# Moving a weight split from the last 33 attention steps into the last ten, and two of its operations to GpSimd

## The chip, the cores and the metric

The kernel runs on one core of one Trainium2 chip. The metric is device time in microseconds (us). The kernel before takes 701.96 us, the median of 3 runs that lie between 701.85 and 702.72.

A core has five engines that each work through an instruction queue of their own, in order, and wait for one another through semaphores: PE (TensorE, matmuls and transposes), DVE (VectorE), ACT (ScalarE), POOL (GpSimd) and SP (SyncE, which here only issues DMA transfers).

## The reference, cut to what matters

```
# attention: 2 batches x 8 heads, 1152 keys, 64 per head, queries averaged in pairs (576)
q_pool = q.reshape(B, H, S // 2, 2, D).mean(axis=3)
attn   = softmax(q_pool @ k.T / sqrt(D))            # with + 1e-09 in the denominator
x      = (attn @ v), heads side by side             # 1152 tokens x 512
# first feed-forward layer (d_ff 2048)
h = x @ w_in
x = where(h > 0, h, exp(min(h, 0)) - 1) @ w_out
# second feed-forward layer (d_ff 1536)
xn  = x / sqrt(mean(x * x) + 1e-06) * rms_g
out = (silu(xn @ w_gate) * (xn @ w_val)) @ w_out2
```

The weights are float64 in DRAM. The kernel reads each as pairs of 32-bit words and builds a float32 from them with integer and float operations; each float32 is then split into a high and a low part, and a product is three matmuls (high by high, low by high, high by low).

## The kernel before

**Attention** runs in 72 steps: eight pairs of heads p (0 to 7) by nine query tiles i (0 to 8). Step n issues, in this order:

- PE: the score matmuls of tile n into the PSUM tile `s` (L279, 6 matmuls, 12 for tile 2 of each p, which serves both heads). There is one `s` buffer, so they wait until DVE has read the scores of tile n-1.
- DVE: `p` (L283), which copies the scores out of `s` and takes their minimum.
- PE: nine transposes of the probabilities of tile n-2 into three PSUM banks `t` (L297). For each bank ACT casts the high part out (`pth`, L305), then DVE subtracts it (`ptl`, L69). There are only three banks, so the transposes of step n+1 wait for the casts and subtractions of step n.
- PE: up to eight matmuls of probabilities by values (L323).
- ACT: the exponential of tile n (L288).
- POOL: the preparation of a later head's q, k or v (`do_prep`), followed by SP's DMA of the next one (`fetch`). The k halves and the v tiles share two buffers (tag `raw`), so SP's DMA for one waits until POOL is done with the tile two places earlier.
- last, `ws.step`, which takes operations from the weight stream.

**The weight stream** (class `Stream`) hands out one operation for each `next`. For a piece of 128 x 512 weights these are, in order: the ACT operation A (`wt`, L113) on the high words; e (`we`, L115) on the low words; then the rest of the piece before it (a marker, the ACT copy of its high part `wh` L141, its low part `wl` on POOL L63); the clamp (L120); the shift (L122); the sign (L124), after which the load of a further piece is issued; and the integer add (L128). That is nine steps of the stream for a piece. The raw words are in two buffers (`wr`, loaded in L90 by SP); `load` issues a piece's DMA ahead, but the first two loads are issued in the same place as the first A. Three pieces can be split before the attention buffers are freed; the stream then stops by itself.

The stream is advanced by L500, one operation in each of the last 33 attention steps, so the three pieces and the float32 of a fourth are built over steps 39 to 71. After attention `early` multiplies with the three pieces, and `elu` advances the stream by two operations at two places of each tile.

The order of every engine's queue is the order in which the program issues; nothing reorders it.

Of the kernel before, what the change touches and what calls it, by code (L numbers as in the profile page):

```python
# [11 lines left out]
ALU = mybir.AluOpType  # L12
# [12 lines left out]
LEAST64, MOST64 = 2.0 ** -18, float.fromhex("0x1.dffffep+13")  # L25
# [13 lines left out]
def tile_kernel(ctx: ExitStack, tc: tile.TileContext, qd, kd, vd, w1d, w2d, wgd, wvd, wod, rgd, outd):  # L39
    nc = tc.nc  # L40
    V, G, T, PE, SP = nc.vector, nc.gpsimd, nc.scalar, nc.tensor, nc.sync
    ctx.enter_context(tc.manual_schedule())
    f = lambda a: a.bitcast(F32)
# [27 lines left out]
    NE, WB = 3, 8  # L71

    class Stream:
# [23 lines left out]
        def work(self):  # L97
            tail = None
            for i in range(len(self.srcs)):
                if tail and not wide:  # L100
                    yield from tail
                self.load(i + 2)
                w = self.raw.pop(i)
                if wide:

                    lo, hi = w[:, :, 0], w[:, :, 1]  # L110
                    e = wp.tile([128, 512], U32, tag="we", name="we", bufs=2)
                    t = wp.tile([128, 512], U32, tag="wt", name="wt", bufs=2)
                    T.activation(out=f(t), in_=f(hi), func=AF.Abs, scale=0.125)  # L113
                    yield
                    V.tensor_scalar(out=f(e), in0=lo, scalar1=2.0 ** -27, scalar2=2.0 ** 25,  # L115
                                    op0=ALU.mult, op1=ALU.add)
                    yield
                    if tail:
                        yield from tail
                    V.tensor_scalar(out=f(t), in0=f(t), scalar1=LEAST64, scalar2=MOST64, op0=ALU.max, op1=ALU.min)  # L120
                    yield
                    V.tensor_scalar(out=t, in0=t, scalar1=3, scalar2=None, op0=ALU.logical_shift_left)  # L122
                    yield
                    V.scalar_tensor_tensor(out=t, in0=hi, scalar=0x80000000, in1=t,  # L124
                                           op0=ALU.bitwise_and, op1=ALU.bitwise_xor)
                    self.load(i + 3)
                    yield
                    V.tensor_tensor(out=t, in0=t, in1=e, op=ALU.add)  # L128
                    w = f(t)
                tail = self.split(i, w)  # L130
                yield
            yield from tail
# [135 lines left out]
    def emit_S(p, i):  # L268
        if i == 0:
            st[p] = ap.tile([128, 4, NPT, 1], F32, tag="st", name="st", bufs=2)  # L270
        s = (tp if (p, i) == (0, 1) else sp).tile([128, 3, 512], F32, tag="s", name="s", bufs=1)
        if i == M:
            parts = [(QD[p, j][:, u, c:c + 128], KD[p, j]) for j, c in ((1, 0), (0, 576)) for u in (0, 1)]
        else:
            j, c, _, _, _ = TILES[i]
            parts = [(QD[p, j][:, u, c:c + 128], KD[p, j]) for u in (0, 1)]
        for n, (a, b) in enumerate(parts):
            for m in range(3):
                PE.matmul(s[:, m, 0:384], lhsT=a, rhs=b[:, 384 * m:384 * m + 384],  # L279
                          start=n == 0, stop=n == len(parts) - 1)  # L280
        pt = P[p, i] = ap.tile([128, 3, 384], F32, tag="p", name="p", bufs=3)

        V.tensor_scalar(out=pt, in0=s[:, :, 0:384], scalar1=-0.0625, scalar2=None,  # L283
                        op0=ALU.mult, op1=ALU.min, accum_out=st[p][:, 0, TILES[i][4], :])

    def emit_exp(p, i):
        pt = P[p, i]
        T.activation(out=pt, in_=pt, func=AF.Exp, scale=-1.0, bias=st[p][:, 0, TILES[i][4], :],  # L288
                     accum_out=st[p][:, 1, TILES[i][4], :])
# [57 lines left out]
    def emit_r(p):  # L347
        s = st[p]
        V.tensor_scalar(out=s[:, 2], in0=s[:, 1], scalar1=1e-9, scalar2=None, op0=ALU.add)
        V.reciprocal(s[:, 3], s[:, 2])  # L350
        hi_pool(rs, s[:, 3, 0:8].to_broadcast([128, 8, 64]))

    def emit_scale(p):

        s, x = st[p], xf[p]
        rb, rm = tbank(), tbank()
        for k in range(4):
            PE.transpose(rb[:, 128 * k:128 * k + 128], rs[:, 2 * k:2 * k + 2, :].rearrange("p a b -> p (a b)"), ident)
        PE.transpose(rm[:, 0:128], s[:, 3, 8, :].to_broadcast([128, 128]), ident)
        xs = ap.tile([128, QS], F32, tag="xs", name="xs", bufs=1)  # L360
        for a, b in ((0, 0), (320, 256)):
            T.copy(xs[:, a:a + 256], rb[:, b:b + 256])
        for j in range(2):
            r = slice(64 * j, 64 * j + 64)
            T.copy(xs[r, 256:320], rm[r, r])
        return xs

    def emit_x(p, xs, a=0, b=QS):
        x = xf[p][:, a:b]
        n, c = divmod(p, 4)  # L370
        h, l = (t[:, c, n * QS + a:n * QS + b] for t in (xh, xl))
        if p < 7:
            G.tensor_tensor(out=x, in0=x, in1=xs[:, a:b], op=ALU.mult)
            hi_pool(h, x)
            lo_pool(l, x, h)
        else:
            V.tensor_tensor(out=x, in0=x, in1=xs[:, a:b], op=ALU.mult)
            T.copy(h, x)
            lo_dve(l, x, h)
# [4 lines left out]
    ws = Stream(w_in[:NE] + [w for hf in range(2) for w in  # L384
                             (w_in[8:16] if hf else w_in[NE:8]) + [w_out[4 * (2 * hf + q) + m] for m in range(4) for q in range(2)]]
                + [w[i] for i in range(12) for w in (wgd, wvd)] + [wod[i] for i in range(12)])
# [4 lines left out]
    def do_prep(u, eng):  # L391
        {"q": prep_q, "k": prep_k, "v": prep_v}[u[0]](*u[1:], raws.pop(u), eng)
# [3 lines left out]
    def fetch(u):  # L396
        if u not in raws:
            raws[u] = load(*u)
# [6 lines left out]
    ns = len(steps)  # L405
# [11 lines left out]
    t = ap.tile([128, 3, 384], F32, tag="p", name="rawq0", bufs=3).rearrange("p a b -> p (a b)")  # L417
    t = t.rearrange("p (u c) -> p u c", u=2)
# [31 lines left out]
    def do_T(step):  # L450
        pt, it = steps[step - LT]
        if avq and any(overwrites(it, a.g) for a in avq):
            assert not any(overwrites(it, a.g) for a in avq[1:])
            avq[0].emit(18)
        emit_T(pt, it)

    def do_AV(k, then):
        while k and avq:
            k -= avq[0].emit(k)
            if avq[0].n < 18:  # L460
                break
            a = avq.pop(0)
            a.finish()
            if a.g is GROUPS[3]:
                then(a.p)

    def after_T(step):
        pt, it = steps[step - LT]
        seen.add((pt, it))
        for g in GROUPS:  # L470
            if it in g["tiles"] and all((pt, t) in seen for t in g["tiles"]):
                avq.append(AV(pt, g))

    for step in range(ns):
        emit_S(*steps[step])
        if step == 1:
            tctx.close()
            tp = actx.enter_context(tc.tile_pool(name="psT", bufs=1, space=PSUM))
            tbank = lambda: tp.tile([128, 512], F32, tag="t", name="t", bufs=3)

        due = [w for w in later if w[0] <= step]
        if step >= LT and not due:
            do_T(step)
        for w in due:
            later.remove(w)
            w[1]()
        do_AV(8, lambda p: later.append((step + 2, lambda: emit_x(p, emit_scale(p)))))
        if step >= LT and due:
            do_T(step)
        emit_exp(*steps[step])  # L490
        if step >= LT:
            if steps[step - LT][1] == NPT - 1:
                emit_r(steps[step - LT][0])
            after_T(step)
        for u in jobs.get(step, []):
            do_prep(u, (ACT[0], lo_pool) if step < 4 and u[0] != "q" else POOL)
            n = order.index(u)
            if n + 1 < len(order):
                fetch(order[n + 1])
        ws.step(0, step >= ns - 33)  # L500


    fb = sp.tile([128, 3, 512], F32, tag="s", name="fb", bufs=1)
# [233 lines left out]
```

## Time and profile before

| what | us |
|---|---|
| time of the profiled execution | 702.4 |
| its span, first to last instruction | 700.6 |
| median of the 3 runs | 701.96 |
| PE busy | 682.1 (97%) |
| DVE busy | 546.2 (78%) |
| ACT busy | 416.0 (59%) |
| POOL busy | 374.9 (54%) |

The span is what lies between the first and the last instruction; the reported time has 1.8 us more around it. Busy time is a sum over the whole span, and an engine's share differs between stages: a stage is read from a table of windows or a timeline. The attention steps end at about 250 us, and the first tile after attention (`elu`) starts at 262.6 us.

### The profile page before, as it was taken

The numbers are of one execution on the slowest core, as the hardware profiler recorded it, in microseconds if no ns is written. First come the engines' busy times: TensorE is split into PE (matmuls) and PEld (weight loads), VectorE is DVE, ScalarE is ACT, GpSimd is POOL, SyncE is SP. The second block draws the span as 40 slices with busy tenths as digits, with TensorE's granted clock in tenths as the row PEclk, the third lists the DMA queues.
The fourth block names the chain that finished last, engine by engine and source line by source line (L and its number), as shares of the span: only waits on it lengthen the run. The fifth ranks groups of instructions, "written<-read, shape, count | busy, mean of one in ns | idle before, by whom it ended". The sixth has DMA issues, their size and how long they took to land.

```text
span 700.6 us, 11340 instructions
## 1 busy us (share of the span) xinstructions
PE 682.1 (97%) x4243; PEld 669.4 (96%) x4243; DVE 546.2 (78%) x897; ACT 416.0 (59%) x855; POOL 374.9 (54%) x326
## 2 busy tenths in 40 slices
PE   7999999999999999996999999999999999999997
PEld 6999999989899999996999999999999999999997
DVE  6988889898999967999988999766999876584000
ACT  5988889889887957765447774434444444342000
POOL 3989788897978405765434545442454443342000
PEclk9999999999999999998999999999999999999999
DMA  5423323433432001222442222200323222232000
GB/s 199 123 85 114 124 86 102 145 116 95 143 114 67 1 31 33 89 90 94 148 142 69 70 83 91 90 1 31 121 91 114 96 91 91 90 101 84 35 35 34
DMA packets 21606, 62.33 MB, mean 89 GB/s; under 512 B 2736, under 2 KB 4784, under 8 KB 21552
## 3 DMA queue, kind: packets, MB, share of 16 engines
q1 hardware_dynamic: 21552, 61.62, 26.4%
q8 instruction: 33, 0.54, 0.3%
q14 instruction: 21, 0.17, 0.1%
HBM read 59.25 MB, written 2.36 MB: 88 GB/s over the span
## 4 chain that ended last, share of the span: by engine, by line
PE 81%; DVE 12%; ACT 3%; POOL 1%; DMA 1%; issue 1%; SPq 0%; DVEq 0%; ACTq 0%; POOLq 0%
PE b L168 17%; PE b L167 17%; PE b L169 17%; PE s L279 10%; PE o L323 9%; PE t L297 8%; DVE p L283 3%; DVE ptl L69 2%; DVE wt L124 2%; DVE wt L122 1%; DVE wt L120 1%; DVE e L187 1%; DMA rawk<-in_k_dram 1%; POOL wl L63 1%; DVE wt L128 1%
## 5 line engine op out<-in xcount | busy, mean ns | idle before, releaser
L167 PE MATMUL b<-xh,wh 128*128 128x384 f32 x468 | 157.4, 336 | 0.6 <-ACT sl L638 0.6
L169 PE MATMUL b<-xh,wl 128*128 128x384 f32 x468 | 157.1, 336 | 0.0
L168 PE MATMUL b<-xl,wh 128*128 128x384 f32 x468 | 157.0, 335 | 0.0
L63 POOL TENSOR_TENSOR wl<-wt,wh 128x512 fp32r<-128x512 f32 x68 | 99.8, 1467 | 72.8 <-ACT wh L141 53.8
L283 DVE TENSOR_SCALAR_CACHE_REDUCE p<-s 128x1152 f32<-128x1152 f32 x72 | 97.4, 1353 | 20.0 <-PE s L279 19.9
L69 DVE TENSOR_TENSOR ptl<-t,pth 128x384 fp32r<-128x384 f32 x216 | 106.6, 549 | 2.7 <-ACT pth L305 2.2
L279 PE MATMUL s<-kd,qt 128*128 128x384 f32 x480 | 99.3, 345 | 5.5 <-DVE p L283 3.8
L305 ACT CAST pth<-t 128x384 fp32r<-128x384 f32 x216 | 89.4, 486 | 23.3 <-PE t L297 22.7
L288 ACT ACTIVATE p<-p,st 128x1152 f32<-128x1152 f32 x72 | 91.4, 1269 | 5.8 <-DVE p L283 5.4
L279 PEld LDWEIGHTS s<-kd,qt 128*128 128x128 f32 x480 | 82.8, 191 | 9.1 <-DVE p L283 4.3
L167 PEld LDWEIGHTS b<-xh,wh 128*128 128x128 f32 x468 | 87.9, 188 | 1.1 <-ACT sl L638 0.9
L168 PEld LDWEIGHTS b<-xl,wh 128*128 128x128 f32 x468 | 87.9, 188 | 0.0
L169 PEld LDWEIGHTS b<-xh,wl 128*128 128x128 f32 x468 | 87.9, 188 | 0.0
L297 PE MATMUL t<-ident,p 128*128 128x128 f32 x648 | 85.5, 275 | 0.2 <-DVE p L283 0.2
L113 ACT ACTIVATE wt<-wr 128x512 f32<-128x512 f32 x68 | 46.0, 676 | 66.6 <-POOL wl L63 50.9
L323 PE MATMUL o<-pth,vd 128*128 128x256 f32 (+1 forms) x288 | 84.4, 315 | 0.0
L124 DVE SCALAR_TENSOR_TENSOR wt<-wr,wt 128x512 uint32<-128x512 uint32 x68 | 80.5, 1184 | 1.8
L297 PEld LDWEIGHTS t<-ident,p 128*128 128x128 f32 x648 | 73.9, 141 | 6.6 <-DVE ptl L69 4.0
L323 PE MATMUL o<-ptl,vd 128*128 128x256 f32 (+1 forms) x288 | 78.4, 295 | 0.0
L63 POOL TENSOR_TENSOR gl<-e,gh 128x384 fp32r<-128x384 f32 x37 | 44.9, 1215 | 45.8 <-ACT gh L188 45.8
L128 DVE CUSTOM_DVE_ANT_0 wt<-wt,we 128x1024 uint16<-128x1024 uint16 x68 | 65.8, 968 | 1.9
L167 PE MATMUL b<-gh,wh 128*128 128x384 f32 x180 | 62.0, 344 | 5.2 <-ACT gh L188 4.6
(113 smaller groups left out, 1317.6 us busy)
## 6 DMA issues: line engine op xcount, KB each, us to landing
wr<-in_w_dram SPq DMA_DIRECT2D x32, 512.0 KB, 3.2
rawk<-in_k_dram SPq DMA_DIRECT2D x32, 288.0 KB, 2.9
rawq<-in_q_dram SPq DMA_DIRECT2D x15, 576.0 KB, 4.0
wr<-in_wg_dram SPq DMA_DIRECT2D x12, 512.0 KB, 3.2
wr<-in_wv_dram SPq DMA_DIRECT2D x12, 512.0 KB, 3.2
wr<-in_wo_dram SPq DMA_DIRECT2D x12, 512.0 KB, 3.2
rawv<-in_v_dram SPq DMA_DIRECT2D x16, 288.0 KB, 2.9
out_dram<-o SPq DMA_DIRECT2D x12, 192.0 KB, 1.8
```

Of the source, the lines that this page charges most:

```text
L63: G.tensor_tensor(out=o, in0=i, in1=f(h), op=ALU.subtract)
L69: V.tensor_tensor(out=o, in0=i, in1=f(h), op=ALU.subtract)
L124: V.scalar_tensor_tensor(out=t, in0=hi, scalar=0x80000000, in1=t, op0=ALU.bitwise_and, op1=ALU.bitwise_xor)
L167: PE.matmul(out, lhsT=wh[:, k, :], rhs=ah, start=first and k == 0, stop=False)
L168: PE.matmul(out, lhsT=wh[:, k, :], rhs=al, start=False, stop=False)
L169: PE.matmul(out, lhsT=wl[:, k, :], rhs=ah, start=False, stop=last and k == 3)
L279: PE.matmul(s[:, m, 0:384], lhsT=a, rhs=b[:, 384 * m:384 * m + 384], start=n == 0, stop=n == len(parts) - 1)
L283: V.tensor_scalar(out=pt, in0=s[:, :, 0:384], scalar1=-0.0625, scalar2=None, op0=ALU.mult, op1=ALU.min, accum_out=st[p][:, 0, TILES[i][4], :])
L288: T.activation(out=pt, in_=pt, func=AF.Exp, scale=-1.0, bias=st[p][:, 0, TILES[i][4], :], accum_out=st[p][:, 1, TILES[i][4], :])
L297: PE.transpose(ps[:, k, :], src[:, 128 * b:128 * b + 128], ident)
L305: T.copy(oh, re(ps))
L323: PE.matmul(self.o[:, 0:self.N], lhsT=v[:, b, :], rhs=(pth, ptl)[u][:, g["buf"], b, g["c0"]:320], start=self.n == 0, stop=self.n == 17)
```

## The change

The e operation and the clamp of the first three pieces go to POOL instead of DVE, and the two bounds of the clamp change places. The stream is advanced by three operations in each of the last ten attention steps (62 to 71) instead of by one in each of the last 33. Line numbers behind L116 are one higher in the changed kernel.

```diff
-                    V.tensor_scalar(out=f(e), in0=lo, scalar1=2.0 ** -27, scalar2=2.0 ** 25,
-                                    op0=ALU.mult, op1=ALU.add)
+                    (G if i < NE else V).tensor_scalar(out=f(e), in0=lo, scalar1=2.0 ** -27, scalar2=2.0 ** 25,
+                                                       op0=ALU.mult, op1=ALU.add)
                     yield
                     if tail:
                         yield from tail
-                    V.tensor_scalar(out=f(t), in0=f(t), scalar1=LEAST64, scalar2=MOST64, op0=ALU.max, op1=ALU.min)
+                    (G if i < NE else V).tensor_scalar(out=f(t), in0=f(t), scalar1=MOST64, scalar2=LEAST64,
+                                                       op0=ALU.min, op1=ALU.max)
...
-        ws.step(0, step >= ns - 33)
+        ws.step(0, 3 * (step >= ns - 10))
```

Three places of the order matter. On SP, at the end of the attention's loads (`rawk`, `rawv` and `rawq` are the k, v and q tiles, `wr` the raw words of the weights), there stands before:

```order
L233 DMA rawv<-in_v_dram 128x576
L224 DMA rawq<-in_q_dram 128x1152
L230 DMA rawk<-in_k_dram 128x576 x2
L90 DMA wr<-in_w_dram 128x1024
L233 DMA rawv<-in_v_dram 128x576
L90 DMA wr<-in_w_dram 128x1024 x27
```

and now:

```order
L234 DMA rawv<-in_v_dram 128x576
L225 DMA rawq<-in_q_dram 128x1152
L231 DMA rawk<-in_k_dram 128x576 x2
L234 DMA rawv<-in_v_dram 128x576
L90 DMA wr<-in_w_dram 128x1024 x32
```

Five loads of weights stood between the attention's loads, the first two of them in step 39; now all 32 stand behind the last of them, the v tile of head 7, 0.

On ACT, around the exponential of step 62 (`p`), there stands before, from the casts of step 62 to those of step 64:

```order
L305 CAST pth<-t 128x3x128 x3
L288 ACTIVATE p,st<-p,st 128x1152
L305 CAST pth<-t 128x3x128 x3
L336 COPY olo<-o 64x320
L338 COPY xf<-o 64x320
L288 ACTIVATE p,st<-p,st 128x1152
L113 ACTIVATE wt<-wr 128x512
L305 CAST pth<-t 128x3x128 x3
```

and now:

```order
L306 CAST pth<-t 128x3x128 x3
L289 ACTIVATE p,st<-p,st 128x1152
L113 ACTIVATE wt<-wr 128x512
L306 CAST pth<-t 128x3x128 x3
L337 COPY olo<-o 64x320
L339 COPY xf<-o 64x320
L289 ACTIVATE p,st<-p,st 128x1152
L306 CAST pth<-t 128x3x128 x3
```

The A operation that stood here was that of the fourth piece; the one that stands here now is that of the first, directly behind the exponential of step 62 and ahead of the casts of step 63.

On DVE, from the scores of step 62 to those of step 64, there stands before:

```order
L283 TENSOR_SCALAR p,st<-s 128x1152
L69 TENSOR_TENSOR ptl<-t,pth 128x3x128 x3
L128 ISA wt<-wt,we 128x1024
L283 TENSOR_SCALAR p,st<-s 128x1152
L69 TENSOR_TENSOR ptl<-t,pth 128x3x128 x3
L283 TENSOR_SCALAR p,st<-s 128x1152
```

and now:

```order
L284 TENSOR_SCALAR p,st<-s 128x1152
L69 TENSOR_TENSOR ptl<-t,pth 128x3x128 x3
L284 TENSOR_SCALAR p,st<-s 128x1152
L69 TENSOR_TENSOR ptl<-t,pth 128x3x128 x3
L123 TENSOR_SCALAR wt<-wt 128x512
L125 SCALAR_TENSOR_TENSOR wt<-wr,wt 128x512
L129 ISA wt<-wt,we 128x1024
L284 TENSOR_SCALAR p,st<-s 128x1152
```

Shift, sign and add of a piece stood in steps of their own; now the three stand together behind the subtractions of step 63, and in the same way in steps 66 and 69 for the second and third piece.

## Rows read from the trace of the kernel before

**Rows 1.** The page: busy time, share of the span and instructions of each engine.

```profile
PE 682.1 (97%) x4243; PEld 669.4 (96%) x4243; DVE 546.2 (78%) x897; ACT 416.0 (59%) x855; POOL 374.9 (54%) x326
```

**Rows 2.** Table of windows: stretch, length, busy PE PEld DVE ACT POOL, clock, DMA, GB/s.

```profile
120.00:140.00 20.00, 20.00 (x147) 19.84 (x146) 16.67 (x33) 16.62 (x36) 16.67 (x16) 1.00 0.37 127
200.00:220.00 20.00, 18.82 (x135) 17.64 (x134) 19.73 (x37) 16.70 (x36) 18.99 (x18) 1.00 0.32 102
```

**Rows 3.** Timeline of DVE, line 349, once per pair of heads: start, length, engine, line.

```profile
101.32 0.16 DVE L349 TENSOR_SCALAR st<-st 128x9 f32<-128x9 f32 x1
...
131.20 0.16 DVE L349 TENSOR_SCALAR st<-st 128x9 f32<-128x9 f32 x1
...
225.87 0.16 DVE L349 TENSOR_SCALAR st<-st 128x9 f32<-128x9 f32 x1
```

**Rows 4.** Timeline of DVE, the scores of steps 35, 38, 62, 65 and 71.

```profile
121.79 1.36 DVE L283 TENSOR_SCALAR_CACHE_REDUCE p<-s 128x1152 f32<-128x1152 f32 x1 [0.21 <-PE s L279]
...
132.79 1.36 DVE L283 TENSOR_SCALAR_CACHE_REDUCE p<-s 128x1152 f32<-128x1152 f32 x1 [1.18 <-PE s L279]
...
216.54 1.34 DVE L283 TENSOR_SCALAR_CACHE_REDUCE p<-s 128x1152 f32<-128x1152 f32 x1
...
227.17 1.36 DVE L283 TENSOR_SCALAR_CACHE_REDUCE p<-s 128x1152 f32<-128x1152 f32 x1 [0.60 <-PE s L279]
...
246.69 1.35 DVE L283 TENSOR_SCALAR_CACHE_REDUCE p<-s 128x1152 f32<-128x1152 f32 x1
```

**Rows 5.** Timeline of POOL, the first k half fetched in a pair's last steps.

```profile
125.66 1.43 POOL L63 TENSOR_TENSOR kd<-rawk,kd 64x576 fp32r<-64x576 f32 x1
```

**Rows 6.** Timeline of SP, the next v tile, and the first two weight loads.

```profile
127.12 0.33 SPq L233 DMA_DIRECT2D rawv<-in_v_dram  x1
...
134.97 1.18 SPq L90 DMA_DIRECT2D wr<-in_w_dram  x2
```

**Rows 7.** DMA issues, whole span: KB each, median us from issue to landing.

```profile
wr<-in_w_dram SPq DMA_DIRECT2D x32, 512.0 KB, 3.2
```

**Rows 8.** DMA issues, 134.5 to 140 us, the first two weight loads alone.

```profile
wr<-in_w_dram SPq DMA_DIRECT2D x2, 512.0 KB, 4.4
```

**Rows 9.** Timeline of ACT, end of step 35's exponential and casts of step 36.

```profile
124.42 0.19 ACT L288 ACTIVATION_READ_ACCUMULATOR p<-p,st 128x1 f32 x1
125.63 1.25 ACT L305 CAST pth<-t 128x384 fp32r<-128x384 f32 x3 [1.02 <-PE t L297]
```

**Rows 10.** Timeline of PE, transposes of step 37, scores of step 38.

```profile
128.32 1.15 PE L297 MATMUL t<-ident,p 128*128 128x128 f32 x9
...
130.48 2.27 PE L279 MATMUL s<-kd,qt 128*128 128x384 f32 x12
```

**Rows 11.** Timeline of DVE, subtractions of step 36.

```profile
126.38 1.48 DVE L69 TENSOR_TENSOR ptl<-t,pth 128x384 fp32r<-128x384 f32 x3
```

**Rows 12.** Instructions on the tile wt: ns min/median/max, first and last start.

```profile
L113 ACT ACTIVATE wt<-wr x68: 648/677/705, 139.0 to 638.6; 128x512 f32<-128x512 f32 x68
...
L122 DVE TENSOR_SCALAR wt<-wt x68: 415/428/1406, 149.0 to 639.8; 128x512 uint32<-128x512 uint32 x68
L124 DVE SCALAR_TENSOR_TENSOR wt<-wr,wt x68: 673/1371/1670, 152.0 to 640.2; 128x512 uint32<-128x512 uint32 x68
L128 DVE CUSTOM_DVE_ANT_0 wt<-wt,we x68: 675/693/1670, 156.0 to 641.0; 128x1024 uint16<-128x1024 uint16 x68
...
L63 POOL TENSOR_TENSOR wl<-wt,wh x68: 1277/1470/1830, 175.8 to 647.1; 128x512 fp32r<-128x512 f32 x68
```

**Rows 13.** Groups of POOL by shape, 0 to 262 us: busy, mean ns, idle before.

```profile
L60 POOL TENSOR_SCALAR rs<-st 128x512 f32<-128x512 f32 x8 | 4.9, 618 | 22.5 <-DVE st L350 13.1 <-PE t L297 9.4
```

**Rows 14.** Timeline of PE, its longest wait, behind attention.

```profile
319.80 0.69 PE L167 MATMUL b<-gh,wh 128*128 128x384 f32 x1 [4.58 <-ACT gh L188]
```

**Rows 15.** Table of windows, PE alone: length, busy, clock, DMA, GB/s.

```profile
320.00:321.00 1.00, 0.49 (x1) 0.50 0.00 0
...
326.00:327.00 1.00, 1.00 (x7) 0.99 0.07 16
```

## The prediction

> **What bounds the kernel now.** I read the page first: PE is busy 97% of the span [rows 1], so a change can only win where PE waits, and lose by making it wait. Next I read the table of windows over attention. From 120 to 140 us PE is busy all 20 us and DVE 16.7; from 200 to 220 us PE falls to 18.8 and DVE rises to 19.7 [rows 2]. So the attention steps are bound by PE until the weight stream starts in step 39, and by DVE while it runs. The timeline of DVE gives the price. Line 349 comes once per pair of heads: 29.88 us apart without the stream (131.20 - 101.32), but 94.67 us for the three pairs that follow, against 3 x 29.88 = 89.64 [rows 3]. The stream costs 5.0 us there.
>
> **What the change removes.** Steps 39 to 61 lose every stream operation, so these steps should run at the undisturbed pace. I carry undisturbed steps forward: the scores of step 35 start at 121.79, so those of step 62, 27 steps on, start at 121.79 + 89.64 = 211.4, against 216.54 now: 5.1 us early. In the same way step 65 would start at 132.79 + 89.64 = 222.4 (227.17 before) and step 71 at 121.79 + 119.52 = 241.3 (246.69 before) [rows 4]. If the moved work cost nothing the kernel would win 5.4 us.
>
> **What it adds, first: a wait for a load at the head of ACT's queue.** The first A now stands in ACT's queue in step 62, and its raw words are loaded by a DMA that is issued in the same step, behind the v tile of head 7, 0. That v tile waits for a buffer that POOL frees when it ends the k half two places earlier. In the undisturbed pair POOL starts that operation at 125.66 and takes 1.43 [rows 5], and SP issues the v tile at 127.12, right behind it [rows 6]. Carried forward this is 216.76, and with 0.33 for its issue the first weight load goes out at 217.1. Before, the first two loads also stood behind a k tile [rows 6], but 4 us ahead of the first A at 139.0 [rows 12]. A load lands 3.2 us after its issue in the median of all 32 [rows 7], and 4.4 in the median of that first pair, which flies together with a k tile [rows 8]. I take 4.1, near the pair's row, because here too two loads fly behind an attention tile and only the first is waited for. So A starts at 221.2 (bounds 220.3 and 221.5).
>
> ACT is ready for A much earlier: the exponential of step 35 ends at 124.61, so that of step 62 ends at 214.25 [rows 9]. ACT stands for 7 us. Behind A are the casts of step 63, which would have started at 125.63 + 89.64 = 215.3 [rows 9]. POOL stands too, with e at its head; behind it are only an addition for the output of pair 6, the reciprocals of that pair and the last v tile, all needed steps later, so I cost its wait at nothing.
>
> PE has slack of about 2 us here: step 63's transposes find free banks, step 64's scores need only DVE. Then step 64's transposes, due at 128.32 + 89.64 = 218.0 [rows 10], need a bank that is cast and subtracted. A takes 0.68 [rows 12] and ends at 221.9; the first cast (a third of 1.25 [rows 9]) and the first subtraction (a third of 1.48 [rows 11]) with their hand-over make 1.0. The transposes start at 222.9: PE waits 4.9 us (4.0 to 5.2).
>
> **What it adds, second: three DVE operations together in steps 63, 66 and 69.** Shift, sign and add cost at least 0.42 + 0.67 + 0.68 = 1.8 us and at most 1.41 + 1.67 + 1.67 = 4.75 [rows 12]; the medians make 2.5. The least and the most differ by whether POOL works at the same time. In steps 63 and 66 POOL has little to do, in step 69 it has the output of pair 6. I take 2.2 for each, between the least and the medians.
>
> - Step 63: the subtractions end at 221.9 + 0.5 + 1.5 = 223.9, the three operations at 226.1, the scores of step 64 (1.36) at 227.45. Only then can PE write the twelve score matmuls of step 65 (2.1, from the length of 2.27 less the tail of the last [rows 10]). Step 65's scores on DVE start at 229.55. That is 2.4 us later than before (227.17), so the 5 us are spent here already.
> - Steps 66 to 71: undisturbed they take 241.3 - 222.4 = 18.9, before 19.5. Two bursts of 2.2 and one e of 0.42 on the fourth piece add 4.8. DVE's own work is 1.36 + 1.48 = 2.84 a step, the step 3.15, so there are 0.3 x 6 = 1.9 us of room, of which two output additions of about 0.4 take 0.8. Of the remaining 1.1 I let 0.8 be used, since a burst must be absorbed within a step. That leaves 4.0, less the 0.6 that these steps lost before: 3.4 us.
> - In step 66 the shift also waits for the clamp on POOL, behind ACT's copy and the low part of the first piece (1.47 [rows 12]). The clamp on POOL is not in the trace; the nearest row is a POOL operation of the same shape with one input, 0.62 [rows 13], at most 1.47. By 0.62 it is done when DVE comes to it; by 1.47 it costs up to 0.8.
>
> **Third: the clock of TensorE.** After its longest wait now, 4.58 us [rows 14], PE ran at a granted clock of 0.50 (1.2 GHz instead of 2.4) until 326 us [rows 15], some 6 us of work at half speed. The wait forecast here is as long. But the half-speed stretch would be mostly under the DVE burst of step 63, where PE waits again; only step 65's matmuls (2.1 more at half speed) lie in the open. I take 1.0, bounds 0 and 3.
>
> **Fourth, the rest.** After step 71 the fourth piece's add (0.68) gives way to its clamp (0.42): -0.2. Its shift, sign and add fall between the first `elu` tiles, where DVE waits for ACT; I cost them at nothing, and at 1.8 if that cover is gone. Products behind attention get their three pieces as before.
>
> **Sum.** 2.4 + 3.4 + 1.0 - 0.2 = +6.6 us. The profiled execution would go from 702.4 to 709.0 and its span from 700.6 to 707.2. Its time is 0.44 above the median of the runs, so I put the sum on the median: 701.96 + 6.6 = 708.6. With the shortest landing, clean bursts, all of the room and no loss of clock it is +1.0 + 2.2 + 0 = +3.2, 705.2; with the long ends, held to what POOL can be busy with, about +11, 713.
>
> A word on the bursts by rule: the Trainium skill, SBUF — State Buffer, "Who interferes with whom", says that DVE and GpSimd share a port pair as an exclusive lock, so that the one that comes second waits for the whole instruction of the other. The rows agree: the sign operation takes 0.67 or 1.37 to 1.67 [rows 12]. By the rule each of the nine burst operations could meet a POOL operation, the second rival below.
>
> **The rivals.**
>
> - *The words are there in time (faster).* With DVE's stream gone, POOL may run ahead of the undisturbed pair and free the v buffer earlier. It decides if the first load goes out before 214.25 - 4.1 = 210.1, seven us earlier than computed. Then only the bursts cost: 3 x 2.2 + 0.42, less the room of 1.1 and about 1.3 of slack in step 63, makes 4.6; against 5.4 won it is -0.8, with clean bursts -2.0. I give 700.6. Against it: the undisturbed pair, with no stream at all, issues its v tile just behind POOL [rows 5, 6]. Chance 0.09.
> - *Every burst meets POOL (slower still).* Then step 69's burst, under the three operations for the output of pair 6, costs 4.75, and steps 63 and 66 some 1 us more in all: 708.6 + 2.5 + 1 = 712. For it: the median sign operation is at 1.37. Against it: POOL has little else in these steps. Chance 0.17.
> - *The gain isn't there.* If the pairs 4 to 6 are slow for another reason than the stream, the 5.0 us stay lost: 713.6. Against it: the step from 29.88 to 31.6 us comes with the first stream operation. Chance 0.03.
> - *The wait is hidden and the rest cancels.* Bursts that are partly absorbed and a wait of under 1 us: 702. Chance 0.04.
>
> **How the numbers follow.** The forecast has 0.67 and its own range is 705 to 711. A measurement of this kernel can tell about 0.2% (1.4 us) from no change. The first rival gives 0.08 to faster and the rest to no change; the fourth gives no change; everything else is slower. So: faster 0.08, same 0.05, slower 0.87. The range 703.5 to 712.5 holds the forecast and most of the second rival, and leaves out the first and third.
>
> **What would show it.** Line 349 of the changed profile should come every 29.9 us up to step 64's. ACT should show one wait of about 7 us for the DMA of the raw words in front of its first A, near 214 us, and PE one of 4 to 5 us for a subtraction near 218, with a lower clock behind it. DVE should show three blocks of shift, sign and add in steps 63, 66 and 69, and PE waits for the scores behind them. Step 65's scores near 229.5, step 71's near 253. The forecast is wrong if ACT's wait is missing or PE's is under 2 us; it is too high if the bursts take 1.8 us each and steps 66 to 71 stay near 21 us.

## The result, and the profile after

The changed kernel takes 712.20 us, the median of 4 runs (711.35 to 713.77). The kernel before, in 4 runs, takes 702.33 (701.85 to 702.72). The ratio is 1.0141, with a 95% interval from 1.0126 to 1.0155: the change makes the kernel 9.9 us slower. The forecast was +6.6 and 708.6; the time lies beyond its own range of 705 to 711 and 0.3 us inside the wider one, 703.5 to 712.5. The profiled span goes from 700.6 to 710.4 us, +9.8.

The page's row of busy times answers to [rows 1]:

```profile
PE 684.7 (96%) x4243; PEld 673.1 (95%) x4243; DVE 543.8 (77%) x891; ACT 415.5 (58%) x855; POOL 376.0 (53%) x332
```

PE does the same 4243 matmuls, yet is busy 2.6 us longer in a span 9.8 us longer. So some 7 us are waits, and some of the busy time is slower matmuls. The list of PE's waits says where, from 212 to 258 us (total, times, longest):

```profile
PE s L280 <- DVE p L284: 5.6, 3, 2.9
PE t L298 <- DVE ptl L69: 4.5, 1, 4.5
```

DVE's timeline, cut to the scores that answer to [rows 4] (steps 62, 65 and 71), with those of step 64 and the burst in front of them (start, length, engine, line, wait in front of it):

```profile
211.36 1.36 DVE L284 TENSOR_SCALAR_CACHE_REDUCE p<-s 128x1152 f32<-128x1152 f32 x1 [0.21 <-PE s L280]
...
221.89 1.48 DVE L69 TENSOR_TENSOR ptl<-t,pth 128x384 fp32r<-128x384 f32 x3 [5.85 <-ACT pth L306]
223.30 0.42 DVE L123 TENSOR_SCALAR wt<-wt 128x512 uint32<-128x512 uint32 x1
223.75 1.31 DVE L125 SCALAR_TENSOR_TENSOR wt<-wr,wt 128x512 uint32<-128x512 uint32 x1
225.09 0.69 DVE L129 CUSTOM_DVE_ANT_0 wt<-wt,we 128x1024 uint16<-128x1024 uint16 x1
225.70 1.35 DVE L284 TENSOR_SCALAR_CACHE_REDUCE p<-s 128x1152 f32<-128x1152 f32 x1
...
229.50 1.36 DVE L284 TENSOR_SCALAR_CACHE_REDUCE p<-s 128x1152 f32<-128x1152 f32 x1 [0.72 <-PE s L280]
...
256.45 1.36 DVE L284 TENSOR_SCALAR_CACHE_REDUCE p<-s 128x1152 f32<-128x1152 f32 x1 [0.65 <-PE s L280]
```

Step 62 starts at 211.36, 5.18 us earlier than before: the gain is there. Step 65 starts at 229.50, 2.33 later than before, and step 71 at 256.45, 9.76 later. The whole loss is made between 215 and 257 us.

The first of the two losses begins in SP's and ACT's queues (SP first, then ACT):

```profile
216.70 0.33 SPq L234 DMA_DIRECT2D rawv<-in_v_dram  x1
217.08 0.91 SPq L90 DMA_DIRECT2D wr<-in_w_dram  x2
```

```profile
213.98 0.19 ACT L289 ACTIVATION_READ_ACCUMULATOR p<-p,st 128x1 f32 x1
220.83 0.66 ACT L113 ACTIVATE wt<-wr 128x512 f32<-128x512 f32 x1 [6.66 <-DMA wr<-in_w_dram]
221.40 1.22 ACT L306 CAST pth<-t 128x384 fp32r<-128x384 f32 x3
```

The loads go out behind the v tile, which answers to [rows 6], and land 3.7 us later. ACT has stood for 6.66 us, and the casts of step 63 behind its A.

PE's timeline shows the four waits and the instructions behind them, and between the second and the third an undisturbed pair of rows. "x6", "x9" and "x12" are runs of matmuls:

```profile
222.51 1.83 PE L298 MATMUL t<-ident,p 128*128 128x128 f32 x9 [4.46 <-DVE ptl L69]
...
227.11 2.35 PE L280 MATMUL s<-kd,qt 128*128 128x384 f32 x12 [0.64 <-DVE p L284]
...
234.48 1.21 PE L280 MATMUL s<-kd,qt 128*128 128x384 f32 x6
235.53 1.15 PE L298 MATMUL t<-ident,p 128*128 128x128 f32 x9
...
239.66 1.77 PE L280 MATMUL s<-kd,qt 128*128 128x384 f32 x6 [2.05 <-DVE p L284]
241.23 2.12 PE L298 MATMUL t<-ident,p 128*128 128x128 f32 x9
...
254.12 2.29 PE L280 MATMUL s<-kd,qt 128*128 128x384 f32 x6 [2.91 <-DVE p L284]
256.21 1.73 PE L298 MATMUL t<-ident,p 128*128 128x128 f32 x9
```

Six score matmuls take 1.21 us undisturbed, 1.77 behind the third wait and 2.29 behind the last. The table of windows for PE has the reason (stretch, length, busy, granted clock, DMA, GB/s):

```profile
223.00:226.00 3.00, 3.00 (x14) 0.54 0.00 0
...
227.00:240.00 13.00, 10.84 (x79) 1.00 0.16 54
240.00:243.00 3.00, 3.00 (x15) 0.55 0.14 57
...
244.00:254.00 10.00, 7.21 (x52) 1.00 0.08 19
254.00:257.00 3.00, 2.88 (x10) 0.50 0.28 111
```

Behind the waits of 4.46, 2.05 and 2.91 us some 3 us follow at or near a granted clock of 0.50, which is 1.2 GHz; then 2.4 GHz comes back. [Rows 15] showed this behind one wait of 4.58. A wait of 2.05 was enough here.

The bursts of steps 66 and 69, and POOL beside them (DVE first, then POOL, whose first line lies beside the sign of step 63):

```profile
236.11 0.43 DVE L123 TENSOR_SCALAR wt<-wt 128x512 uint32<-128x512 uint32 x1 [0.21 <-POOL wt L120]
236.58 1.02 DVE L125 SCALAR_TENSOR_TENSOR wt<-wr,wt 128x512 uint32<-128x512 uint32 x1
237.64 0.69 DVE L129 CUSTOM_DVE_ANT_0 wt<-wt,we 128x1024 uint16<-128x1024 uint16 x1
...
249.34 0.89 DVE L123 TENSOR_SCALAR wt<-wt 128x512 uint32<-128x512 uint32 x1
250.27 1.79 DVE L125 SCALAR_TENSOR_TENSOR wt<-wr,wt 128x512 uint32<-128x512 uint32 x1
252.10 0.69 DVE L129 CUSTOM_DVE_ANT_0 wt<-wt,we 128x1024 uint16<-128x1024 uint16 x1
```

```profile
223.64 0.86 POOL L340 TENSOR_TENSOR xf<-xf,olo 64x320 f32<-64x320 f32 x1 [1.34 <-ACT xf L339]
...
236.16 0.90 POOL L115 TENSOR_SCALAR we<-wr 128x512 f32<-128x512 uint32 x1
...
247.77 1.43 POOL L374 TENSOR_TENSOR xf<-xf,xs 128x576 f32<-128x576 f32 x1
249.29 0.67 POOL L60 TENSOR_SCALAR xh<-xf 128x576 fp32r<-128x576 f32 x1
250.04 1.47 POOL L63 TENSOR_TENSOR xl<-xf,xh 128x576 fp32r<-128x576 f32 x1
```

The burst of step 63 takes 2.42 us of work, that of step 66 takes 2.14, that of step 69 takes 3.37. The sign (L125) lies beside a POOL operation in all three; in step 69 the shift lies beside POOL's cast as well.

### The profile page after: what moved, and what is told of

Same layout as the page of the kernel before. It is cut to its first block, busy times and chain, and to the rows that moved or that the text cites. A ratio compares the mean times of both kernels' runs of the same rounds, so it can differ in the third digit from the quotient of the medians.

```text
span 710.4 us, 11376 instructions
## 1 busy us (share of the span) xinstructions
PE 684.7 (96%) x4243; PEld 673.1 (95%) x4243; DVE 543.8 (77%) x891; ACT 415.5 (58%) x855; POOL 376.0 (53%) x332
## 4 chain that ended last, share of the span: by engine, by line
PE 79%; DVE 9%; POOL 4%; ACT 4%; DMA 2%; issue 1%; SPq 1%; POOLq 0%; DVEq 0%; ACTq 0%
PE b L169 17%; PE b L168 17%; PE b L170 17%; PE s L280 10%; PE o L324 9%; PE t L298 8%; DVE wt L125 2%; DVE wt L123 1%; DVE p L284 1%; DVE e L188 1%; DMA rawk<-in_k_dram 1%; DVE wt L129 1%; DVE wt L120 1%; POOL wl L63 1%; DVE ptl L69 1%
## 5 line engine op out<-in xcount | busy, mean ns | idle before, releaser
L298 PE MATMUL t<-ident,p 128*128 128x128 f32 x648 | 87.6, 279 | 4.9 <-DVE ptl L69 4.5
L298 PEld LDWEIGHTS t<-ident,p 128*128 128x128 f32 x648 | 75.7, 143 | 11.7 <-DVE ptl L69 8.7
L125 DVE SCALAR_TENSOR_TENSOR wt<-wr,wt 128x512 uint32<-128x512 uint32 x68 | 80.6, 1185 | 1.9
```

Of the source, the lines that this page charges most:

```text
L298: PE.transpose(ps[:, k, :], src[:, 128 * b:128 * b + 128], ident)
```

## The experiments

Ratios are to the kernel before, run on the same chip in between. Kernels of different groups are compared by their ratios.

**1. The load issued earlier.** The changed kernel, with the first two loads issued in step 56, six steps ahead of the step that wants them:

```diff
+        if step == ns - 16:
+            ws.load(2)
         ws.step(0, 3 * (step >= ns - 10))
```

> The changed kernel with one thing undone: the first two raw loads are issued six steps earlier (step 56), so that the first A finds its words landed. Theory (the wait for the load, its burst and the half clock behind it make the first 7 us of loss): ACT's wait of 6.7 us and PE's of 4.5 us go, the burst of step 63 keeps about 1.1 us of its 2.4 because DVE and PE have 1.3 us of slack there; step 65's scores start near 223.5 instead of 229.5, steps 66 to 71 stay as they are; 706 us. Rival (the bursts alone decide, the wait only hides the first of them): the first burst is paid in full with a half clock of its own behind it, 709.5 us or more.

Measured: 710.26 us (709.30 to 711.66), ratio 1.0106 [1.0082, 1.0130]. ACT's wait for the load is gone, but the ratio is only 0.0035 below the changed kernel's, and the two intervals overlap. The rival's size is right, but the reason is one that neither theory had. DVE's timeline shows it, and POOL's behind it:

```profile
220.36 0.43 DVE L123 TENSOR_SCALAR wt<-wt 128x512 uint32<-128x512 uint32 x1 [2.92 <-POOL wt L120]
```

```profile
216.71 0.67 POOL L60 TENSOR_SCALAR kd<-rawk 128x576 fp32r<-128x576 f32 x1
217.47 1.42 POOL L63 TENSOR_TENSOR kd<-rawk,kd 64x576 fp32r<-64x576 f32 x1
218.98 0.65 POOL L115 TENSOR_SCALAR we<-wr 128x512 f32<-128x512 uint32 x1
219.71 0.61 POOL L120 TENSOR_SCALAR wt<-wt 128x512 f32<-128x512 f32 x1
```

The clamp takes only 0.61, but POOL is late: the last k half stands ahead of e and the clamp in its queue, and there is no gap until they are done. DVE waits 2.92 for it, the burst follows, PE waits and runs at half speed: the twelve score matmuls of step 65 take 4.21 us instead of 2.27 [rows 10].

```profile
224.10 4.21 PE L280 MATMUL s<-kd,qt 128*128 128x384 f32 x12 [3.91 <-DVE p L284]
```

**2. The operations back on DVE.** The changed kernel, with e and the clamp on DVE:

```diff
-                    (G if i < NE else V).tensor_scalar(out=f(e), in0=lo, scalar1=2.0 ** -27, scalar2=2.0 ** 25,
+                    V.tensor_scalar(out=f(e), in0=lo, scalar1=2.0 ** -27, scalar2=2.0 ** 25,
...
-                    (G if i < NE else V).tensor_scalar(out=f(t), in0=f(t), scalar1=MOST64, scalar2=LEAST64,
+                    V.tensor_scalar(out=f(t), in0=f(t), scalar1=MOST64, scalar2=LEAST64,
```

> The changed kernel with e and the clamp of the first three pieces back on DVE; three operations a step in the last ten steps stay. Theory (DVE is what the late steps wait for): DVE now stands behind the first load too, the scores of step 63 come after the clamp at about 222, and each later piece adds 0.8 to 1.9 us of DVE; about 716 us. Rival (GpSimd's operations hold up DVE at the shared port): without them the bursts are shorter, 711 us or less.

Measured: 711.46 us (710.69 to 711.96), 1.0124 [1.0106, 1.0143]; not to be told from the changed kernel, and near the rival's 711, not the theory's 716. DVE now stands behind the load itself, and PE's wait for the scores behind it is 6.25 us, the longest of all runs:

```profile
220.18 0.43 DVE L115 TENSOR_SCALAR we<-wr 128x512 f32<-128x512 uint32 x1 [6.66 <-DMA wr<-in_w_dram]
```

Step 65 starts 0.53 us later than in the changed kernel (230.03). From there to step 71 it takes 23.94 us instead of 26.95, although DVE does more. Its bursts keep clear of POOL more often (the sign takes 0.69 in steps 63 and 66, 1.79 in step 69), and 1.9 of the 3.0 us come in front of steps 69 and 71, which in the changed kernel follow PE's half speed. Here PE's wait in step 66 is shorter, and the granted clock behind it stays at 1.00 (window 236 to 253 us):

```profile
239.55 1.32 PE L280 MATMUL s<-kd,qt 128*128 128x384 f32 x6 [1.41 <-DVE p L284]
```

Of the 2.48 us that it is ahead at step 71 (253.97), 0.9 go in its last transposes and the way to `elu` (271.34 against 272.94), and the spans differ by 0.6 in the end. The last 1.0 lies behind attention; the spans of the changed kernel's own four runs go from 709.6 to 712.0, so it can't be told from the spread of the runs.

**3. Both edits at once** (the early load, and the operations on DVE):

> The changed kernel with both waits of its first piece undone at once: the first two raw loads go out in step 56, and e and the clamp are back on DVE; three operations a step in the last ten steps stay. In the profile with the early loads alone, DVE's first shift stood 2.9 us for the clamp, which was behind the last k half in POOL's queue. Theory (either wait hides the other, so both must go): no wait over 1 us in steps 62 and 63, step 65's scores near 224, steps 66 to 71 as with the operations on DVE alone (24 us), about 703.5 us. Rival (the three bursts are the loss, the waits are only where it shows): as the early loads alone, 709 us or more.

Measured: 706.74 us (705.78 to 708.21), 1.0059 [1.0045, 1.0074], between the two. No wait for the load or for POOL is left. The single edits bring 0.0035 and 0.0017 in the ratio, both together 0.0082; with intervals as wide as these the ratios alone don't show that this is more than the sum of 0.0052. The start of step 65 does: against the changed kernel it comes 1.15 us earlier with the early load, 0.53 later with the operations on DVE, and 2.79 earlier (226.71) with both. So two waits stand in each other's shadow: ACT's for the load and DVE's for POOL's queue. The steps from 65 to 71 take 23.98 us, as in experiment 2. What is left over the kernel before, 4 us, shows as three PE waits behind the bursts, the longest of 2.6, two of them with half speed behind them:

```profile
PE s L280 <- DVE p L284: 6.4, 3, 2.6
```

**4. The bursts taken apart, on DVE.** The third kernel, with the load three steps earlier still, and the stream over the last 13 steps, so that shift, sign and add have a step each and e and the clamp share one:

```diff
-        if step == ns - 16:
+        if step == ns - 19:
             ws.load(2)
-        ws.step(0, 3 * (step >= ns - 10))
+        if step >= ns - 13:
+            ws.step(0, [3, 1, 1, 1, 6, 1, 1, 1, 6, 1, 1, 1, 5][step - ns + 13])
```

> The run with early loads and e and the clamp on DVE, with one thing changed: the same 30 operations stand in the last 13 steps so that shift, sign and add have a step each, and e and the clamp share one. The amount of DVE work is the same. Theory (three or more operations in one step are paid in full, and the waits that they make PE take cost its clock on top; single ones are partly covered): 4 to 5 us less, about 702 us, and no stretch of half clock in the attention steps. Rival (the amount of work in the last steps counts, not how it lies): 706.5 us.

Measured: 701.99 us (701.45 to 703.23, 10 runs), 0.9983 [0.9973, 0.9992]. That is the theory's time. In the ratio it is 0.0076, or 5.3 us, under experiment 3, for the same operations on the same engine. The table of windows for PE from 200 to 260 us, of experiment 4 and then of the changed kernel:

```profile
200.00:260.00 60.00, 57.54 (x405) 1.00 0.18 57
```

```profile
200.00:260.00 60.00, 49.94 (x326) 0.91 0.22 74
```

PE's longest wait from 200 to 250 us is 1.1 us, and the granted clock stays at 1.00. Which part of the 5.3 us is the burst's own length and which the clock it costs, this run doesn't separate.

**5. The bursts taken apart, with the operations on POOL.** The same order of steps and the same early load in the changed kernel.

> The changed kernel with the first two loads in step 53 and the stream's 30 operations in the last 13 steps so that shift, sign and add stand in three steps of their own each (3, 1, 1, 1, 6, 1, 1, 1, 6, 1, 1, 1, 5 operations a step). Theory (a burst of three in one step is paid in full because PE and DVE can't make it up, single ones are partly covered, and PE never stands long enough to lose its clock): about 1.2 us a piece, 701 us. Rival (only the amount of DVE work in the last steps counts): as with the early loads alone, 706 us.

Measured: 701.79 us (700.66 to 702.95, 12 runs), 0.9989 [0.9979, 0.9999], near the theory's 701, and 8.5 us under experiment 1, which ran in the same group. The stream also starts three steps earlier than there, so that other work of POOL stands ahead of the clamps; the 8.5 us are not shown to be the bursts' alone. One wait of DVE for the clamp is left, 1.71 us, and PE's longest is 0.7:

```profile
226.76 0.43 DVE L123 TENSOR_SCALAR wt<-wt 128x512 uint32<-128x512 uint32 x1 [1.71 <-POOL wt L120]
```

**6. The other half of the change alone.** The kernel before, with e and the clamp on POOL and one operation in each of the last 33 steps.

> The other half of the change alone: e and the clamp of the first three pieces on GpSimd, the stream in the last 33 steps, one operation a step, as before. Theory (POOL's lag is what counts): the clamp stands in tile 5, behind q and k of the next pair, and the shift in tile 6 waits for it, slower by 2 to 6 us: 704 to 708 us. Rival (DVE's time is what the stream costs, and a third of it goes): 700.5 us.

Measured: 703.21 us (702.21 to 704.82, 10 runs), 1.0005 [0.9992, 1.0017]. No difference, which neither theory gave. No wait of DVE for the clamp is listed in this trace, though a v tile stands right ahead of all three clamps on POOL: they end at 147.70, 179.98 and 211.59, and the shifts start at 148.97, 180.02 and 211.63, the last two with nothing to spare:

```profile
179.37 0.61 POOL L120 TENSOR_SCALAR wt<-wt 128x512 f32<-128x512 f32 x1
```

```profile
180.02 0.43 DVE L123 TENSOR_SCALAR wt<-wt 128x512 uint32<-128x512 uint32 x1
```

Nor does the relief of DVE bring anything: it waits 9.0 us for PE's scores from 120 to 252 us where it waited 8.1 before.

**7. A shift by three steps.** The kernel before, with the stream over the last 30 steps instead of 33:

```diff
-        ws.step(0, step >= ns - 33)
+        ws.step(0, step >= ns - 30)
```

> The kernel before with one number changed: the stream starts in step 42 instead of 39, still one operation a step, all on DVE as before. It moves the shift, sign and add of each piece from tiles 6, 7 and 8 of a pair to tiles 0, 1 and 2, where undisturbed DVE waits 0.6, 1.2 and 0.5 us for the scores. Theory (what an operation costs is decided by the room of the step that it stands in): most of the 5.0 us that the stream costs in pairs 4 to 6 go, 698 us. Rival (DVE's total work decides): no change, 702 us.

Measured: 700.11 us (698.60 to 701.77, 12 runs), 0.9963 [0.9952, 0.9975]: 2.5 us less, where the theory had 4 and the rival nothing. ACT's first A waits 1.79 us for its load.

**8. The same with an early load** (`ws.load(2)` in step 35).

> The kernel before with the stream's start moved to step 42, and the first two raw loads issued seven steps ahead of it (step 35). In the run without the early loads ACT waited 1.8 us for them and step 44's scores came 2.5 us late. Theory (that wait is a cost of the same kind as in the change, and it is all that the early loads take away): 2 us less than with the start in step 42 alone, 698 us. Rival (the wait is absorbed within the pair): 700 us.

Measured: 700.22 us (699.63 to 701.63, 6 runs), 0.9970 [0.9959, 0.9982]. The wait is gone and the profiled span is 1.3 us shorter than in 7, but the ratios can't be told apart: the rival's result.

**9. The same, with e and the clamp on POOL.** It differs from experiment 8 in the engine of the two operations alone.

> As the run with the start in step 42 and early loads, and e and the clamp of the first three pieces on GpSimd as in the change. Theory (POOL lags by up to 5 us behind the step in which it is given an operation, while it prepares k halves; the clamp stands in tile 8 behind one of these, and the shift in the next step on DVE waits for it): PE and DVE wait 1 to 3 us a pair more than without it, 701 to 705 us. Rival (it relieves DVE of 0.8 to 1.9 us a piece): 697 us or less.

Measured: 709.93 us (708.16 to 711.52), 1.0098 [1.0083, 1.0112]: 9.7 us over experiment 8, which ran on the same chip. The direction is the theory's, the size is more than it gave. DVE's list of waits from 120 to 252 us, and POOL's queue at the first of them:

```profile
DVE wt L123 <- POOL wt L120: 10.4, 3, 3.9
```

```profile
159.19 0.66 POOL L115 TENSOR_SCALAR we<-wr 128x512 f32<-128x512 uint32 x1
159.80 0.70 POOL L60 TENSOR_SCALAR kd<-rawk 128x576 fp32r<-128x576 f32 x1
160.58 1.43 POOL L63 TENSOR_TENSOR kd<-rawk,kd 64x576 fp32r<-64x576 f32 x1
162.10 0.61 POOL L120 TENSOR_SCALAR wt<-wt 128x512 f32<-128x512 f32 x1
```

The clamp of each piece stands behind a k half in all three pairs, and costs 2.7 to 3.9 us of DVE's time. Experiment 6 had the same operations three steps earlier, and no wait. So what an operation on POOL costs here is the queue ahead of it, not its own 0.61 us.

**10. Operations placed by hand where DVE has room.** On DVE, with the early load: five operations in steps 53, 62 and 66, one or two in others.

```diff
+        if step == ns - 37:
+            ws.load(2)
-        ws.step(0, step >= ns - 33)
+        ws.step(0, {42: 1, 44: 2, 45: 1, 46: 1, 47: 1, 51: 1, 53: 5, 54: 1, 55: 1, 56: 1,
+                    60: 1, 62: 5, 63: 1, 64: 1, 65: 1, 66: 5, 71: 1}.get(step, 0))
```

> A version meant to beat the others: the kernel before with the first two loads in step 35, and each piece's DVE operations placed by hand in the tiles where undisturbed DVE waits for the scores: e and the clamp before tile 0's (0.6 us of wait), the shift before tile 1's (0.6), the sign before tile 2's (1.2), the add before tile 3's (0.5). Theory (an operation costs what goes beyond the room of its step): of the 0.9 us that e still cost at tile 4 of each pair most goes, 698 to 699 us. Rival (the clamp, with e ahead of it and POOL at work, costs as much there as e did before): 700 us, as with the start in step 42.

Measured: 700.47 us (700.02 to 701.91), 0.9960 [0.9947, 0.9973]: the rival's time. It beats the kernel before, as experiments 7 and 8 do, and none of the three beats the others measurably. In step 44 e takes 1.23 and the clamp 0.89 us on DVE, since POOL prepares a head beside them, and that step and its like in the next pairs take 4.6 us.

## Why the prediction was right, and where its sum was short

**Right: the gain.** Step 62 was put at 211.4 and came at 211.36. The third rival, that the 5 us aren't there, is out.

**Right: the first wait and its way to PE.** The loads were put at 217.1 (217.08), A at 221.2 (220.83), PE's wait at 4.9 (4.46), and step 65's scores at 229.55 (229.50). The single terms of this step partly made up for one another: the load landed in 3.7 us and not 4.1, the burst took 2.4 and not 2.2, and the twelve score matmuls 2.4 and not 2.1. Experiment 1 shows that this wait wasn't needed for the loss: with it gone, step 65 starts at 228.35, only 1.15 us earlier. The prediction had put POOL's wait at nothing. That was true of the changed kernel, where ACT's wait hides it, but the list had missed that POOL is itself late.

**The step that failed in size: "3.4 us" for steps 66 to 71.** At the undisturbed pace these steps take 18.9; here they take 26.95, so 8.1 more, where 4.0 stood. Their scores start at 232.77, 238.25, 241.47, 245.61, 252.71 and 256.45, and the same steps of the pair before, in the same trace, give each its undisturbed length. Three parts:

- The room of 0.8 us was not used. Steps 67, 68 and 70, behind the bursts, come 2.51, 0.20 and 3.37 late, 6.1 together; the bursts and the wait for the clamp make 2.14 + 0.21 + 3.37 = 5.7. Only the single e, 0.42, was absorbed. A burst longer than the room of its own step runs PE dry, and PE, which is the bound, doesn't get this back in the next. Experiment 4 tests it: the same operations spread over more steps bring experiment 3's 1.0059 down to 0.9983. They aren't free: from step 35 to step 71 experiment 3 takes 128.99 us and experiment 4 123.88, against 119.52 at the undisturbed pace, so 4.4 of 9.5 us stay.
- The burst of step 69 met POOL's work for the output of pair 6 and took 3.37 instead of 2.2. This is the part of the second rival that came true; the bursts of steps 63 (2.42) and 66 (2.14) stayed near 2.2, though their signs met POOL too. The Trainium skill, SBUF — State Buffer, "Who interferes with whom", has the second of two overlapping operations wait where DVE reads two SBUF inputs. The sign operation does, and took 1.31 beside a POOL operation of 0.86, 1.02 beside one of 0.90 and 1.79 beside one of 1.47, against 0.69 in experiment 2 where POOL was free: the trace agrees. The sign ends 0.54 to 0.56 us after POOL's operation each time, a little less than its own 0.69.
- The other 2.0 are PE at half speed behind the second and third wait: step 69 comes 1.21 late, with transposes of 2.12 instead of 1.15, and step 71 comes 0.78 late, with scores of 2.29 instead of 1.21.

**The clock, right in kind and put in the wrong place.** 1.0 us was given to step 65's matmuls behind the longest wait. There the half speed lay under the burst, and those matmuls took 2.35 (2.27 undisturbed). The shorter waits behind the bursts cost the clock too, in the open, and the forecast had no clock term there. Each brought some 3 us of work at half speed, where [rows 15] had shown some 6.

**The tail** was put at -0.2 and came out near 0: the first operation of `elu` starts 10.34 later than before, against 9.76 for step 71, since the last transposes run at half speed as well (1.73 instead of 1.15), and about 0.5 comes back later. The fourth piece's three operations under the `elu` tiles cost nothing, as said.

With these sizes the sum is 2.3 up to step 65, 7.4 up to step 71 and 0 behind it: 9.7, against 9.8 in the spans. Not tried by itself is the clock: no run kept the waits and removed the half speed, so its 2.0 us are read from the rows and not isolated. Experiments 2 and 3 come nearest: behind waits of 1.41 and 1.42 us in step 66 the clock stayed at 1.00, and step 69 came 3.00 us behind step 68 in both, against 4.14 here and 2.93 undisturbed.

**The rivals.** "The words are there in time" did not come by itself; experiment 1 made it come, and it doesn't win 1.3 us as worked out but loses 7.6, because POOL's queue was not in it. "Every burst meets POOL" gave 712, which is the measured time, but by another way: the sign met POOL in all three bursts, yet the bursts took 7.9 us together, where the rival had 3.5 more than the forecast's 6.6. That the number agrees is luck, and so is part of the wide range's having held: its upper end was set for this rival.

## What to carry to other kernels

Before an operation goes to an engine with idle time, read what stands ahead of it in that engine's queue in that step: here three clamps of 0.61 us, moved together with their e, cost 0 or 9.7 us for the kernel by the steps in which they stood. Room on a second engine is counted per step; work that is put together in one step runs the bound engine dry, while the same work spread over thirteen steps cost half as much. And where a load's wait at the head of a queue is taken away, look for the wait behind it: two waits that cover each other give little when one of them is removed.

## What was not expected of the hardware

- PE's granted clock fell to 0.50 behind a wait of only 2.05 us, and about 3 us of work at that clock followed each wait of 2.05 to 4.46 in the changed kernel. Waits of up to 1.1 us in experiment 4, and of 1.41 and 1.42 in experiments 2 and 3, left it at 1.00.
- An operation with one input, e or the clamp, took 0.65 and 0.61 us on POOL and 0.42 on DVE alone, but 1.23 and 0.89 on DVE in step 44 of experiment 10, beside POOL's work, so that the place of such an operation matters on either engine.
